# Attention, routed experts and a gated layer on one core: in the slots of the experts, only the splits of weights stand under conditions

## Chip, core and metric

One core of a Trainium2 chip runs the whole program in one launch. The metric is the device time of one execution in microseconds (us); lower is better.

## The reference

Three layers run one behind the other. The attention layer (batch 4, 8 heads, 576 positions, 64 per head) is causal softmax attention mixed with a memory term. Its output is taken as 2304 rows of 512 numbers and goes through a mixture of 8 experts, of which each row uses the one with the highest logit. The result goes through a gated layer with 1536 hidden columns. The part that the change touches is the second:

```python
for e in range(E):                       # E = 8
    mask = e_idx == e                    # e_idx = argmax(x @ w_gate)
    h = np.maximum(x[mask] @ w1[e], 0.0) # w1[e]: 512 x 1024
    ye = h @ w2[e]                       # w2[e]: 1024 x 512
    out[mask] = gate_w[mask, None] * eom[mask, e, None] * ye
```

## The kernel before

**Stages.** The program has a stage of attention and routing (to about 290 us in the profile), a stage of the experts (294 to 620 us) and a gated stage (to the end). The change is in the stage of the experts, in the method `experts`.

**Slots.** Rows are sorted by expert and cut into tiles of 128 rows, with padding where an expert's rows don't fill a tile. One tile is one slot; there are at least 18 (`FULL`) and at most 25 (`SLOTS`), and 23 run with these inputs. The program is written out for all slots; those from 18 on stand inside nested conditions (`more`). All slots use the same two weight tiles in on-chip memory, `W1` and `W2`. Which expert a slot belongs to is known only when the program runs: `another(s)` reads a bit that says whether slot s has another expert than slot s - 1. The condition is evaluated by every engine in its own queue. Here it holds for seven slots (1, 5, 6, 13, 14, 20 and 21, as the profile shows).

**Splits.** Products are made exact enough by splitting each operand into a high part (a copy in a shorter format, made by ACT) and a low part (the rest, made by DVE), and adding three products: high x high, high x low, low x high. An expert's weights are eight pieces of 128 x 1024: pieces 0 to 3 are `W1`, 4 to 7 are `W2`. `split_hi(n)` (line 1185, ACT) and `split_lo(n)` (line 1192, DVE) fill them from the tiles `raw0` to `raw7`; when both are done, the next expert's piece is loaded into the same `raw` tile from SP's queue (`load`, line 1162). So the weights of the next expert wait in `raw` while the present one is used.

**A slot.** `load_x` fetches the rows two slots ahead by an indirect transfer on POOL's queue (lines 1275, 1277). `layer1(n, ...)` is 12 products for half n of the hidden columns (line 1292); `relu(n)` writes `h` (DVE, line 1297); `h_turn(n)` transposes `h` on PE (line 1234) into `pT`; `h_keep(n, 0)` and `h_keep(n, 1)` make its high part (ACT, line 1306) and low part (DVE, line 1304). `layer2(s, n, ...)` is 12 products into `pY` (line 1313): m = 0 to 3 take the high parts of h and of the weights, 4 to 7 the low part of the weights, 8 to 11 the low part of h. `x_turn(s + 1)` and `x_keep(s + 1, ...)` (lines 1234, 1242, 1240) prepare the next slot's rows. `store_y` scales the result on ACT (line 1322) and stores it from SP's queue (line 1323). In slots 13 to 15 a finished tile of results in `yo` is also turned and kept for the gated stage.

**Conditions.** Each slot has two of them, each with an arm for a new expert and an arm for the same one (`either`). The arm `first_half_new` holds the splits of pieces 4 to 7, the keeping of the first half of h and the second ReLU, in one written order; `first_half` holds the same without splits. `second_half_new` and `second_half` do so for pieces 0 to 3 of the next slot's expert, the keeping of the second half of h and of the next x. An arm is one block: the engines run what stands in it in that order, and nothing from outside stands between.

**Gated conversions.** The weights of the gated layer come as 64-bit numbers. Six pieces (`SOON`) are converted during the slots, through the tile `early`, in three steps per piece: `small` (ACT, line 1204) and two conversions on DVE (1211, 1213); two more conversions (1215, 1217); a split (ACT 1229, DVE 1227) and the load of the next piece into `early`. Step k is in slot k, from slot 0 on.

**Order.** The stage is in an order written out by hand (`tc.manual_schedule`); each engine runs its own instructions in the order of the text, and waits where an operand or a buffer isn't ready.

Of the kernel before, what the change touches and what calls it, by code (L numbers as in the profile page):

```python
# [26 lines left out]
NE = 8  # L27
# [10 lines left out]
SOON = 6  # L38
SLOTS = 25
FULL = NT  # L40
# [1077 lines left out]
class Experts:  # L1118
# [126 lines left out]
    def experts(self, rt, gather):  # L1245
        tc, nc = self.tc, self.nc
        V, xn, ids = nc.vector, rt.xn, rt.ids
        with ExitStack() as ctx:
# [6 lines left out]
            xh, xl = (t[:, 0 : 4 * P].rearrange("p (c t) -> p c t", c=4) for t in self.yT)  # L1255
            hh, hl = ([t[:, (4 + 4 * n) * P : (8 + 4 * n) * P] for n in range(2)] for t in self.yT)
            pX, pH, pT, pY = self.ps
            marks = {}

            def value(t, lo, hi, **more):  # L1260
                return nc.values_load_multi_w_load_instructions(t, min_val=lo, max_val=hi, bass_reorder=False, **more)[1][0]
# [1 line left out]
            def only_sp(t, s, top):  # L1263
                return value(t[0:1, s : s + 1], 0, top, engines=[mybir.EngineType.SP])

            def another(s):

                k, b = divmod(s, BITS)
                if k not in marks:
                    marks[k] = value(rt.marks[0:1, k : k + 1], 0, 2**BITS - 1)  # L1270
                return ((marks[k] >> b) & 1) > 0
# [10 lines left out]
            def x_turn(s):  # L1282
                self.turn_rows(pX[s % 2], xn[s % 2])

            def x_keep(s, lo):
                self.keep_rows(pX[s % 2], (xh, xl), 0, lo)
# [9 lines left out]
            def relu(n):  # L1296
                nc.vector.tensor_scalar(h, pH[n], 0.0, None, ALU.max)  # L1297

            def h_turn(n):
                self.turn_rows(pT[n], h)  # L1300

            def h_keep(n, lo):
                if lo:
                    nc.vector.tensor_tensor(hl[n], pT[n], hh[n].bitcast(F32), ALU.subtract)  # L1304
                else:
                    nc.scalar.activation(hh[n], pT[n], AF.Copy)  # L1306
# [18 lines left out]
            def part(n):  # L1325
                self.split_hi(n)
                self.split_lo(n, V)

            def next_loads(s, ns):
                e = only_sp(rt.then, s, NE - 1)  # L1330
                for n in ns:
                    self.load(n, ds(e, 1))

            def first_half(s):

                h_keep(0, 0)
                h_keep(0, 1)
                relu(1)

            def first_half_new(s):  # L1340
                part(4)
                part(5)
                self.split_hi(6)
                h_keep(0, 0)
                h_keep(0, 1)
                relu(1)
                self.split_lo(6, V)
                part(7)
                next_loads(s, range(4, 8))

            def second_half(s):
                h_keep(1, 0)
                h_keep(1, 1)
                if s + 1 < SLOTS:
                    x_keep(s + 1, 0)
                    x_keep(s + 1, 1)

            def second_half_new(s):
                part(0)
                h_keep(1, 0)  # L1360
                h_keep(1, 1)
                part(1)
                x_keep(s + 1, 0)
                x_keep(s + 1, 1)
                part(2)
                part(3)
                next_loads(s + 1, range(4))

            def either(s, new, old, at):
                if not 0 < at < SLOTS:  # L1370
                    old(s)
                    return
                with tc.If(another(at)) as changed:
                    new(s)
                with changed.Else():
                    old(s)

            def slot(s):
                m, step = divmod(s, 3)
                turned = s - 13 if 13 <= s < 16 else None  # L1380
                load_x(s)
                layer1(0, range(12))
                relu(0)
                if m < SOON and step == 0:
                    self.small(m)
                layer1(1, range(6))
                h_turn(0)
                layer1(1, range(6, 12))
                either(s, first_half_new, first_half, s)
                if m < SOON:  # L1390
                    if step < 2:
                        self.convert(m, 2 * step)
                        self.convert(m, 2 * step + 1)
                    else:
                        self.split(m, 0)
                        self.split(m, 1, V)
                        if m + 1 < SOON:
                            self.load_mix(m + 1, self.early)
                layer2(s, 0, range(6))
                h_turn(1)  # L1400
                layer2(s, 0, range(6, 12))
                if s + 1 < SLOTS:
                    x_turn(s + 1)
                either(s, second_half_new, second_half, s + 1)
                if turned is not None:
                    self.turn_rows(pX[s % 2], self.yo[:, turned * DM : (turned + 1) * DM])
                    for i in range(2):
                        self.keep_rows(pX[s % 2], self.second, turned, i)
                layer2(s, 1, range(12))
                store_y(s)  # L1410
                if s in (11, 15):
                    self.load_rows(3 * (s == 15), 3)
# [309 lines left out]
```

## Time and profile before

| | |
|---|---|
| time, median of 3 runs | 1091.81 us (1091.31 to 1094.24) |
| the profiled execution's own time | 1091.38 us |
| its span in the profile | 1089.2 us |
| PE busy | 1009.7 us, 93% |
| DVE busy | 544.7 us, 50% |
| ACT busy | 456.8 us, 42% |
| POOL busy | 216.7 us, 20% |
| mean of the 16 DMA engines | 96 GB/s |

Times of single instructions and slots come from the one profiled execution; its span is the time from its first to its last instruction. PE is the engine of the products (PEld its loads of weights), DVE the vector engine, ACT the scalar engine, POOL the general one, SP the one that issues most transfers. An engine counts as busy while an instruction runs; conditions and register reads are not counted.

### The profile page before, as it was taken

Reading aid. Unit: us, or ns where it says so; the run is one execution under the profiler, and the core shown is the slowest. Engines: PE = TensorE matmul, PEld = TensorE weight load, DVE = VectorE, ACT = ScalarE, POOL = GpSimd, SP = SyncE. Lnnn points to the kernel's source line nnn. Section 1 sums busy time; section 2 is a strip of 40 time slices with the busy share of each in tenths; the row PEclk is TensorE's granted clock in tenths of the full one; section 3 lists DMA queues with packets and bytes.
Section 4 is the critical chain, followed back from the end, with each engine's and each line's share of the span. In section 5 each row is a group of like instructions: output and inputs, shape, how many; then the busy total and the mean of one; then the engine's idle time right before and its main releaser. Section 6 shows DMA issues by size and latency. Waiting matters only on the chain. (4 is left out here: it accounts for less than half of the span.)

```text
span 1089.2 us, 17370 instructions
## 1 busy us (share of the span) xinstructions
PE 1009.7 (93%) x5873; PEld 860.6 (79%) x5873; DVE 544.7 (50%) x1301; ACT 456.8 (42%) x1047; POOL 216.7 (20%) x353
## 2 busy tenths in 40 slices
PE   4889998999579889988998999999999999999997
PEld 3667776777457668867886799999999999999996
DVE  5887877774753653356437399952121121221112
ACT  4888777875342442245226265532211221221211
POOL 8786456530600100011000000000100100100101
PEclk9999999999689999999999999999999999999999
DMA  7667435230553471157218466500200100100000
GB/s 128 137 106 183 106 80 113 68 105 2 186 186 112 140 267 59 59 185 251 69 46 265 131 203 189 166 29 1 78 10 1 59 1 1 59 1 1 29 1 29
DMA packets 114840, 104.66 MB, mean 96 GB/s; under 512 B 71664, under 2 KB 89072, under 8 KB 114736
## 3 DMA queue, kind: packets, MB, share of 16 engines
q1 hardware_dynamic: 111264, 92.11, 30.2%
q0 software_dynamic: 3472, 11.30, 3.1%
q8 instruction: 48, 0.79, 0.3%
q14 instruction: 56, 0.46, 0.1%
HBM read 87.89 MB, written 15.50 MB: 95 GB/s over the span
## 5 line engine op out<-in xcount | busy, mean ns | idle before, releaser
L1529 DVE TENSOR_TENSOR G<-G,pT 128x384 f32<-128x384 f32 (+1 forms) x74 | 40.1, 542 | 247.7 <-PE pT L1515 241.2
L1313 PE MATMUL pY<-W,xh 128*128 128x512 f32 x368 | 103.2, 413 | 18.6 <-ACT W L1185 13.4
L1561 POOL DMA_INDIRECT out_dram<-yo,rows x18 | 17.5, 973 | 455.0 <-ACT yo L1557 364.0
L1536 ACT ACTIVATE Gh<-G 128x384 fp32r<-128x384 f32 (+1 forms) x74 | 38.2, 516 | 159.2 <-DVE G L1529 159.0
L1292 PE MATMUL pH<-W,xh 128*128 128x512 f32 x368 | 98.1, 399 | 2.8 <-ACT xh L1242 2.8
L1313 PEld LDWEIGHTS pY<-W,xh 128*128 128x128 f32 x368 | 66.2, 192 | 35.4 <-ACT W L1185 18.1
L1525 ACT ACTIVATE G<-pH 128x384 f32<-128x384 f32 x72 | 35.5, 492 | 124.5 <-PE pH L1515 124.4
L436 ACT ACTIVATE Sm<-Sm,mx 128x512 f32<-128x512 f32 (+3 forms) x144 | 83.7, 587 | 7.3 <-DVE mx L428 6.9
L1292 PEld LDWEIGHTS pH<-W,xh 128*128 128x128 f32 x368 | 70.0, 191 | 19.7 <-ACT xh L1242 3.2
L1306 ACT ACTIVATE xh<-pT 128x512 fp32r<-128x512 f32 x46 | 27.5, 598 | 122.5 <-PE pT L1234 106.4
L1297 DVE TENSOR_SCALAR h<-pH 128x512 f32<-128x512 f32 x46 | 31.5, 686 | 89.3 <-PE pH L1292 89.3
L1192 DVE TENSOR_TENSOR W<-raw,W 128x1024 fp32r<-128x1024 f32 x59 | 71.1, 1237 | 2.1 <-ACT W L1185 1.0
L428 DVE CUSTOM_DVE_ANT_0 Sm<-Sp,mask 128x512 f32<-128x512 f32 (+3 forms) x144 | 64.5, 482 | 14.3 <-PE T L480 6.9
L480 PE MATMUL T<-ident,Sm 128*128 128x128 f32 x400 | 61.9, 282 | 7.8 <-DVE xT L524 3.1
L318 ACT ACTIVATE pt<-T 128x512 f32<-128x512 f32 (+4 forms) x138 | 55.8, 447 | 30.1 <-PE T L480 28.8
L1185 ACT ACTIVATE W<-raw 128x1024 fp32r<-128x1024 f32 x60 | 60.6, 1050 | 0.3 <-ACT xh L1306 0.3
L480 PEld LDWEIGHTS T<-ident,Sm 128*128 128x128 f32 x400 | 43.9, 141 | 21.3 <-DVE xT L524 5.0
L1304 DVE TENSOR_TENSOR xl<-pT,xh 128x512 fp32r<-128x512 f32 x46 | 31.7, 690 | 57.1 <-ACT xh L1306 57.1
L1534 DVE TENSOR_TENSOR Gl<-G,Gh 128x384 fp32r<-128x384 f32 (+1 forms) x74 | 40.3, 545 | 32.7 <-ACT Gh L1536 32.7
L1292 PE MATMUL pH<-W,xl 128*128 128x512 f32 x184 | 56.7, 410 | 0.0
L1277 POOL DMA_INDIRECT xn<-x_dram,kept x23 | 24.1, 1047 | 155.3 <-PE pX L1234 154.8
L1313 PE MATMUL pY<-W,xl 128*128 128x512 f32 x184 | 50.4, 396 | 0.0
(355 smaller groups left out, 2254.2 us busy)
## 6 DMA issues: line engine op xcount, KB each, us to landing
raw<-in_moe_w_dram SPq DMA_DIRECT2D x68, 512.0 KB, 4.4
y_dram<-y SPq DMA_DIRECT2D x23, 256.5 KB, 5.3
vn<-in_v_dram SPq DMA_DIRECT2D x40, 128.0 KB, 2.6
raw<-in_moe_w_gate_dram SPq DMA_DIRECT2D x10, 512.0 KB, 3.8
raw<-in_moe_w_val_dram SPq DMA_DIRECT2D x10, 512.0 KB
raw<-in_moe_w_out_dram SPq DMA_DIRECT2D x10, 512.0 KB, 3.5
qn<-in_q_dram SPq DMA_DIRECT2D x32, 128.0 KB, 3.3
kn<-in_k_dram SPq DMA_DIRECT2D x32, 128.0 KB, 2.7
```

The source lines that it names most:

```text
L318: self.nc.scalar.activation(out, in_, AF.Copy)
L428: self.nc.vector.tensor_tensor_reduce(out=self.Sm[pi, n][:, k0:k1], in0=self.Sp[pi, c][:, j if n < 8 else si, 0 : k1 - k0], in1=mask, scal ...
L436: self.nc.scalar.activation(self.Sm[pi, n], self.Sm[pi, n], AF.Exp, scale=-1.0, bias=self.mx[pi, n][:, si : si + 1], accum_out=self.sums[p ...
L480: nc.tensor.transpose(T[:, o * 128 : (o + 1) * 128], self.Sm[pi, n][:, k0 : k0 + 128], self.ident)
L1185: self.nc.scalar.activation(self.hi_lo(n)[0], self.first[n] if n in self.first else self.raw[n], AF.Copy)
L1192: eng.tensor_tensor(lo[:, o : o + w], t[:, o : o + w], hi.bitcast(F32)[:, o : o + w], ALU.subtract)
L1292: nc.tensor.matmul(pH[n], lhsT=a[:, m % 4, :], rhs=self.W1[:, c : c + 512], start=(m == 0), stop=(m == 11))
L1313: nc.tensor.matmul(pY[s % 2], lhsT=a[n][:, k * P : (k + 1) * P], rhs=self.W2[:, c : c + 512], start=(n == 0 and m == 0), stop=(n == 1 and ...
L1525: nc.scalar.activation(G[g, f][0], pp[g, f, 0], AF.Sigmoid)
L1529: nc.vector.tensor_tensor(t, t, p, ALU.mult)
L1534: nc.vector.tensor_tensor(l, t, hi.bitcast(F32), ALU.subtract)
L1536: nc.scalar.activation(hi, t, AF.Copy)
```

## The change

- The splits alone stand under conditions, in five blocks per slot, without an else: piece 4 and the high parts of 5, 6, 7; the low parts of 5 and 6 and the loads of 4, 5, 6; the low part of 7 and its load; pieces 0 and 1 of the next expert with their loads; pieces 2 and 3 with theirs. Slot 0 has the last two of these alone.
- What belongs to h, x and the second ReLU stands outside the conditions.
- The next x is turned right behind the second turn of h, six products earlier.
- Step k of the gated conversions is in slot k + 1; slot 17 has the last two steps.
- The number of the expert to load is read by SP at the start of each slot, not inside the arms.

```diff
--- before.py
+++ after.py
@@ -1255,7 +1255,7 @@
             xh, xl = (t[:, 0 : 4 * P].rearrange("p (c t) -> p c t", c=4) for t in self.yT)
             hh, hl = ([t[:, (4 + 4 * n) * P : (8 + 4 * n) * P] for n in range(2)] for t in self.yT)
             pX, pH, pT, pY = self.ps
-            marks = {}
+            marks, following = {}, {}
 
             def value(t, lo, hi, **more):
                 return nc.values_load_multi_w_load_instructions(t, min_val=lo, max_val=hi, bass_reorder=False, **more)[1][0]
@@ -1326,82 +1326,81 @@
                 self.split_hi(n)
                 self.split_lo(n, V)
 
-            def next_loads(s, ns):
-                e = only_sp(rt.then, s, NE - 1)
+            def changed(s):
+
+                return tc.If(another(s)) if 0 < s < SLOTS else None
+
+            def loads(s, ns):
                 for n in ns:
-                    self.load(n, ds(e, 1))
-
-            def first_half(s):
-
+                    self.load(n, ds(following[s], 1))
+
+            def early(k):
+
+                m, step = divmod(k, 3)
+                if step == 0:
+                    self.small(m)
+                if step < 2:
+                    self.convert(m, 2 * step)
+                    self.convert(m, 2 * step + 1)
+                else:
+                    self.split(m, 0)
+                    self.split(m, 1, V)
+                    if m + 1 < SOON:
+                        self.load_mix(m + 1, self.early)
+
+            def slot(s):
+                ends, begins = 0 < s + 1 < SLOTS, 0 < s
+                turned = s - 13 if 13 <= s < 16 else None
+                if ends:
+                    following[s + 1] = only_sp(rt.then, s + 1, NE - 1)
+                load_x(s)
+                layer1(0, range(6))
+                if begins:
+                    with changed(s):
+                        part(4)
+                        for n in (5, 6, 7):
+                            self.split_hi(n)
+                layer1(0, range(6, 12))
+                relu(0)
+                layer1(1, range(3))
+                if begins:
+                    with changed(s):
+                        self.split_lo(5, V)
+                        self.split_lo(6, V)
+                        loads(s, (4, 5, 6))
+                layer1(1, range(3, 6))
+                h_turn(0)
                 h_keep(0, 0)
                 h_keep(0, 1)
+                layer1(1, range(6, 12))
                 relu(1)
-
-            def first_half_new(s):
-                part(4)
-                part(5)
-                self.split_hi(6)
-                h_keep(0, 0)
-                h_keep(0, 1)
-                relu(1)
-                self.split_lo(6, V)
-                part(7)
-                next_loads(s, range(4, 8))
-
-            def second_half(s):
+                layer2(s, 0, range(3))
+                if begins:
+                    with changed(s):
+                        self.split_lo(7, V)
+                        loads(s, (7,))
+                for k in ([] if not 0 < s < FULL else [s - 1] if s < FULL - 1 else range(s - 1, 3 * SOON)):
+                    early(k)
+                layer2(s, 0, range(3, 6))
+                if ends:
+                    with changed(s + 1):
+                        part(0)
+                        part(1)
+                        loads(s + 1, (0, 1))
+                h_turn(1)
+                if ends:
+                    x_turn(s + 1)
                 h_keep(1, 0)
                 h_keep(1, 1)
-                if s + 1 < SLOTS:
+                if ends:
                     x_keep(s + 1, 0)
                     x_keep(s + 1, 1)
-
-            def second_half_new(s):
-                part(0)
-                h_keep(1, 0)
-                h_keep(1, 1)
-                part(1)
-                x_keep(s + 1, 0)
-                x_keep(s + 1, 1)
-                part(2)
-                part(3)
-                next_loads(s + 1, range(4))
-
-            def either(s, new, old, at):
-                if not 0 < at < SLOTS:
-                    old(s)
-                    return
-                with tc.If(another(at)) as changed:
-                    new(s)
-                with changed.Else():
-                    old(s)
-
-            def slot(s):
-                m, step = divmod(s, 3)
-                turned = s - 13 if 13 <= s < 16 else None
-                load_x(s)
-                layer1(0, range(12))
-                relu(0)
-                if m < SOON and step == 0:
-                    self.small(m)
-                layer1(1, range(6))
-                h_turn(0)
-                layer1(1, range(6, 12))
-                either(s, first_half_new, first_half, s)
-                if m < SOON:
-                    if step < 2:
-                        self.convert(m, 2 * step)
-                        self.convert(m, 2 * step + 1)
-                    else:
-                        self.split(m, 0)
-                        self.split(m, 1, V)
-                        if m + 1 < SOON:
-                            self.load_mix(m + 1, self.early)
-                layer2(s, 0, range(6))
-                h_turn(1)
                 layer2(s, 0, range(6, 12))
-                if s + 1 < SLOTS:
-                    x_turn(s + 1)
-                either(s, second_half_new, second_half, s + 1)
+                if ends:
+                    with changed(s + 1):
+                        part(2)
+                        part(3)
+                        loads(s + 1, (2, 3))
                 if turned is not None:
                     self.turn_rows(pX[s % 2], self.yo[:, turned * DM : (turned + 1) * DM])
                     for i in range(2):
```

## Rows read from the trace of the kernel before

**Rows 1.** The page, part 1: busy time, share of the span, instructions.

```profile
PE 1009.7 (93%) x5873; PEld 860.6 (79%) x5873; DVE 544.7 (50%) x1301; ACT 456.8 (42%) x1047; POOL 216.7 (20%) x353
```

**Rows 2.** Waits of PE, 294 to 620 us: us in total, times, longest us.

```profile
PE pY L1313 <- ACT W L1185: 13.4, 14, 1.7
PE pT L1234 <- DVE W L1192: 9.3, 7, 1.4
PE pY L1313 <- ACT xh L1306: 5.2, 1, 5.2
```

**Rows 3.** Windows of slots 0, 1, 2, 4, 5, 6: length, engines busy, clock, DMA.

```profile
294.23:318.11 23.88, 17.00 (x61) 13.19 (x61) 10.93 (x22) 6.13 (x8) 2.25 (x4) 0.77 0.60 204
318.11:332.70 14.59, 12.95 (x62) 10.05 (x60) 9.10 (x11) 6.27 (x8) 1.52 (x3) 1.00 0.70 230
332.70:345.19 12.49, 12.49 (x61) 10.19 (x60) 3.96 (x6) 3.01 (x5) 1.26 (x3) 1.00 0.26 87
...
357.69:372.11 14.42, 12.74 (x62) 10.24 (x60) 9.01 (x11) 6.28 (x8) 1.66 (x3) 1.00 0.34 95
372.11:388.64 16.53, 13.23 (x61) 10.09 (x60) 12.95 (x14) 10.58 (x13) 1.44 (x3) 1.00 0.89 297
388.64:403.25 14.61, 12.99 (x62) 10.05 (x60) 8.57 (x11) 6.82 (x9) 1.26 (x3) 1.00 0.87 293
```

**Rows 4.** Timeline of PE in slot 3: start us, us, instruction.

```profile
349.40 0.60 PE L1234 MATMUL pT<-ident,h 128*128 128x128 f32 x4
...
352.63 0.60 PE L1234 MATMUL pT<-ident,h 128*128 128x128 f32 x4
...
354.81 2.10 PE L1313 MATMUL pY<-W,xh 128*128 128x512 f32 x8
356.75 1.10 PE L1313 MATMUL pY<-W,xl 128*128 128x512 f32 x4
```

**Rows 5.** Timeline of PE in slot 15: x, then `yo`, are turned.

```profile
520.89 0.60 PE L1234 MATMUL pX<-ident,xn 128*128 128x128 f32 x4
521.33 0.60 PE L1234 MATMUL pX<-ident,yo 128*128 128x128 f32 x4
521.69 2.10 PE L1313 MATMUL pY<-W,xh 128*128 128x512 f32 x8
```

**Rows 6.** Timeline of slot 5, in brackets what ended an idle time.

```profile
373.03 2.94 ACT L1185 ACTIVATE W<-raw 128x1024 fp32r<-128x1024 f32 x3
...
378.58 0.68 DVE L1297 TENSOR_SCALAR h<-pH 128x512 f32<-128x512 f32 x1
...
379.18 2.35 DVE L1192 TENSOR_TENSOR W<-raw,W 128x1024 fp32r<-128x1024 f32 x2
381.44 0.68 DVE L1227 TENSOR_TENSOR Wx<-cv_a,Wx 128x512 fp32r<-128x512 f32 x1
381.58 0.66 PE L1234 MATMUL pT<-ident,h 128*128 128x128 f32 x4 [1.33 <-DVE W L1192]
...
382.05 1.22 DVE L1192 TENSOR_TENSOR W<-raw,W 128x1024 fp32r<-128x1024 f32 x1
```

**Rows 7.** Timeline of ACT in slot 0, then windows of all engines there.

```profile
306.37 0.66 ACT L1204 ACTIVATE cv_a<-early 128x512 f32<-128x512 f32 x1 [12.20 <-DMA early<-in_moe_w_gate_dram]
...
306.00:310.00 4.00, 2.43 (x6) 1.94 (x7) 2.05 (x4) 2.09 (x3) 0.00 (x0) 0.50 0.00 0
310.00:312.00 2.00, 2.00 (x9) 1.62 (x8) 1.22 (x1) 0.61 (x2) 0.00 (x0) 0.51 0.00 0
```

**Rows 8.** Groups by line: busy us, mean ns of one, idle before.

```profile
L1217 DVE SCALAR_TENSOR_TENSOR cv_a<-early,cv_a 128x512 int32<-128x512 int32 x6 | 4.2, 692 | 0.2
...
L1211 DVE TENSOR_SCALAR cv_a<-cv_a 128x512 f32<-128x512 f32 x26 | 10.5, 418 | 0.0
```

**Rows 9.** The page, part 6: transfers, KB each, median us to landing.

```profile
raw<-in_moe_w_dram SPq DMA_DIRECT2D x68, 512.0 KB, 4.4
```

**Rows 10.** Waits, 619 to 624 us: PE's queue at a condition not taken.

```profile
PE pH L1515 <- PEq L1416: 0.5, 1, 0.5
```

## The prediction

> **What bounds the kernel now.** I read the page first, then PE's waits in the stage of the experts, then that stage cut into slots, then slots 3, 5 and 0 instruction by instruction. The page shows PE busy 93% of the span [rows 1], so a gain can only come from time in which PE stands still. The profiled execution took 1091.38 us, 2.2 us more than its span of 1089.2; the median of the runs shown is 1091.81, 0.4 above. My sum is made against 1091.4.
>
> The stage runs from 294.2 to 620.1 us: 23 slots. A slot in which nothing changes takes 12.49 us, and PE is busy in all of it [rows 3]: it cannot become shorter unless work is removed, and none is. The slots that are longer are slot 0 and those around the seven changes of expert (the changes are at slots 1, 5, 6, 13, 14, 20 and 21).
>
> PE's waits in the stage [rows 2] have three causes that this change can touch:
> - 14 waits, 13.4 us, of the second-layer products for an ACT instruction of line 1185, and 7 waits, 9.3 us, of the transposes of h for a DVE instruction of line 1192. That is two of the first and one of the second for each change.
> - one wait of 5.2 us for line 1306, in slot 0.
>
> Slot 5 shows what the first kind is. The ReLU writes h at 378.58, two splits of weights follow, and the transpose that reads h, and no weight, starts at 381.58, right behind the end of the splits [rows 6]. So PE does not wait for its operand; it waits for the end of the conditional arm that the operand was made in. That is the mark of it: the releaser is a line whose result is not read.
>
> What it costs is better read from lengths of slots than from idle time, since PE also drains and refills: slots 4, 5 and 6 are 1.93, 4.04 and 2.12 us over 12.49 [rows 3], 8.1 for two changes, 4.04 for one. Slots 12 to 14 and 19 to 21 repeat this, and slots 0 and 1 hold one more change: 7 x 4.04 = 28.3 us. In slot 13 a turn of `yo` fills 0.44 us of it [rows 5], which leaves 27.9.
>
> Slot 0 is 23.88 us long [rows 3]. ACT stands at line 1204 until 306.37, 12.2 us, for the transfer into `early` [rows 7]; behind it in ACT's queue is the copy of h that PE waits 5.2 us for. [...] So the gated conversion costs 7.4 us.
>
> **The change, part by part.**
>
> *h and x kept outside the conditions.* The copies and subtractions of h and x and the second ReLU now stand outside every arm, so their readers need not wait for splits that stand in the same arm. Gain: at most the 27.9 us. A split itself still has to be done before its first reader, so I lay the new order of slot 5, the fullest (it ends one change and begins another), against the places where a slot without waits wants things: the transposes of h at 4.2 and 7.4 us, the last twelve products at 9.6, and the four of them that read the low half of h at 11.6 [rows 4], counted from 345.19.
> ACT: a split costs 0.98 [rows 6]. The first starts 0.9 into the slot, as now [rows 6]; it does 4, 5, 6, 7 to 4.8, then the copy of h to 5.4; wanted at 6.0 (the turn at 4.2, then six products of 0.24). Then splits 0 and 1 to 7.9, h to 8.5, x to 9.1, splits 2 and 3 to 11. Nothing is late.
> DVE: a split costs 1.17, a small step (ReLU, subtraction) 0.6 [rows 6]. Splits 2 and 3 of the slot before reach to about 1.4 by the same steps, and ACT's part of split 4 to 1.9; split 4 to 3.1; ReLU to 3.7, in time for 4.2; splits 5 and 6 to 6.1; subtraction of h and ReLU to 7.3, wanted 7.4 less about 0.1 for the handover: 0.15 late; split 7 to 8.5; two conversions at 0.69 [rows 8] to 9.9; splits 0 and 1 to 12.2; the subtraction of h to 12.9. That is wanted at 11.6, and PE has by then lost nothing else: about 1.5 us late with the handover. DVE's busy time agrees: 12.95 us in slot 5 [rows 3], less one conversion step and plus two, 13.6, against 12.49 of PE.
> Slot 13 has the two shorter conversions, 0.42 each [rows 8], and the turn of `yo`: 1.5 - 0.54 - 0.44, some 0.6 late there, and, since DVE also subtracts the kept rows, 0.6 in slot 14. Slot 20 has no conversion: 0.2. The 0.15 at the second ReLU comes seven times: 1.0. Left over: 1.5 + 0.6 + 0.6 + 0.2 + 1.0 = 3.9.
>
> *Five conditions instead of two, without an else.* 45 conditions become 112 (now two in a slot and one in slot 0, then five and two), and every engine passes each. In the trace DVE leaves an arm and starts the conversion behind it at 381.44 without a gap, and enters the next arm 0.61 later, the spacing of one step [rows 6]; and PE shows no idle time in slot 2, though it passes two conditions there [rows 3]. So I take nothing. Cover: on DVE and ACT the instruction still running, and in unchanged slots the room that the six products behind each turn leave (1.4 us, of which the copy of h takes 0.6); on PE the products queued. The other bound is the one row in which PE's queue itself is the releaser, a condition not taken with nothing behind it: 0.5 us [rows 10]. Without cover the 67 added ones would cost 67 x 0.5, some 34 us.
> [...]
>
> *Conversions from slot 1.* The same instructions, one slot later; the load into `early` keeps its place, so the wait of 12.2 us falls away with the 7.4 us. Later loads of `early` are still issued a slot ahead of their reader. What is late next is slot 17, which now holds two steps: ACT must wait for DVE's two conversions (about 8.6), split, and copy h behind that, about 0.9 us after PE wants it. In slot 0 the first read of the marks by PE and ACT moves to the middle of the slot, where less lies ahead of it: 0.4 taken, between nothing and twice the 0.5 of [rows 10], since no row shows it by itself.
>
> *The turn of x behind the second turn of h.* The same four transposes, six products earlier, so POOL may fetch the next x that much earlier; nothing waits for it. Two turns in a row cost 0.44 + 0.36 where `yo` follows x [rows 5]: up to 0.08 us more than one by itself, against one change-over less; 0.02 taken, 0.4 over 22 slots.
>
> *Loads and SP.* The same eight loads for each change, each behind its own split, as before; SP reads the next expert in every slot, but its address is wanted only when split 4 is done, 3 us into the slot. A load lands 4.4 us after issue [rows 9], and has 8 us or more until its split, even between slots 5 and 6. Nothing.
>
> **The sum.** 27.9 + 7.4 = 35.3 to be had; less 3.9 (DVE), 0.9 (slot 17), 0.4 (marks), 0.4 (turns) = 29.7. 1091.4 - 29.7 = 1061.7 us. The products of the gated stage keep their order and are only shifted.
>
> **The rivals.**
> - *DVE carries the arms.* In changed slots DVE has no slack any more, so an uncovered arm costs there what it costs. Seven changes, five arms each, up to 0.5 us: up to 17.5 us, 1062 to 1079. For it: DVE's 13.6 against 12.49. Against it: the gapless 381.44. Chance 0.17.
> - *The waits stay.* If the condition itself, and not the place of the copy within it, holds the reader back, only slot 0 gains: 1084. For it: every wait of this kind in the trace stands behind an arm. Against it: the delay ends exactly with a split. Chance 0.07.
> - *The branches bind PE (the other side).* If PE's queue has no lead at the added conditions, each costs 0.5 us: 1061.7 + 34 = 1096. It decides from 29.7 / 67 = 0.44 us per condition. For it: the added ones stand three products behind a wait, where the lead is shortest. Against it: the 45 of now cost nothing that shows. Chance 0.07. [...]
>
> **How the numbers follow.** The forecast holds 1056 to 1067 (from all 35.3 recovered to 5 us of small waits): chance 0.66. The rivals take 0.17, 0.07 and 0.07; 0.03 is left for no change. The range 1056 to 1076 takes in the forecast and most of the first rival. A measurement tells about 0.3% (3 us) from no change: faster 0.90, same 0.03, slower 0.07.
>
> **What the profile after would show.** Right: waits of PE for lines 1185 and 1192 nearly gone, slots 4 and 6 at about 12.6, slot 5 at about 14.1 with PE waiting for DVE's subtraction, slot 0 at about 15 (23.88 - 7.4 - 1.93 + 0.4) with no wait at 1204 and no fall of the granted clock inside it, and 12.5 in the rest. Wrong, if unchanged slots are longer than 12.6 (branches), if slots 5, 13 and 20 reach 15 or more (DVE's arms), or if transposes of h still end their wait with a split.

## The result, and the profile after

The changed kernel takes 1060.53 us (median of 4 runs, 1058.03 to 1061.86), the kernel before, run beside it, 1092.28 (4 runs, 1091.31 to 1094.24). The ratio is 0.9703, its 95% interval 0.9684 to 0.9723. The profiled execution of the changed kernel took 1060.34 us, 1058.6 of them span. First its page, part 1, which answers to [rows 1]; PE's instructions are as many as before:

```profile
PE 1005.1 (95%) x5873; PEld 861.6 (81%) x5873; DVE 544.7 (51%) x1301; ACT 455.0 (43%) x1047; POOL 221.2 (21%) x353
```

The waits of PE over the whole stage, which answer to [rows 2]:

```profile
PE pH L1292 <- ACT xh L1242: 3.0, 1, 3.0
PE pY L1313 <- DVE xl L1304: 1.2, 2, 0.9
```

The 14 waits for line 1185, the 7 for line 1192 and the one for line 1306 are gone. The first of the two rows stands at the very start of the stage, for the first turned x; the kernel before has it too, with 2.8 us. The other is new: PE waits in slots 5 and 13 for DVE's subtraction of h.

Windows of slots 0, 1, 2, 4, 5 and 6 of the changed kernel, as in [rows 3]:

```profile
296.53:311.20 14.67, 14.67 (x61) 11.98 (x61) 9.34 (x20) 5.58 (x7) 2.47 (x4) 0.84 0.84 294
311.20:323.68 12.48, 12.48 (x62) 10.26 (x60) 9.04 (x12) 6.73 (x9) 1.26 (x3) 1.00 0.95 320
323.68:336.17 12.49, 12.49 (x61) 10.23 (x60) 4.75 (x7) 2.37 (x4) 1.26 (x3) 1.00 0.15 51
...
348.67:361.17 12.50, 12.50 (x61) 10.23 (x60) 7.36 (x10) 6.83 (x9) 1.26 (x3) 1.00 0.22 81
361.17:374.89 13.72, 12.78 (x61) 10.12 (x60) 13.13 (x16) 10.07 (x12) 2.77 (x3) 1.00 0.96 328
374.89:387.38 12.49, 12.49 (x61) 10.20 (x60) 10.09 (x12) 6.68 (x9) 2.12 (x3) 1.00 0.91 319
```

All 23 slots (us; slots that are not listed lie between 12.46 and 12.50 in both kernels):

| slot | 0 | 1 | 4 | 5 | 6 | 12 | 13 | 14 | 15 | 17 | 19 | 20 | 21 | 22 |
|---|---|---|---|---|---|---|---|---|---|---|---|---|---|---|
| before | 23.88 | 14.59 | 14.42 | 16.53 | 14.61 | 14.43 | 16.53 | 15.03 | 12.94 | 12.50 | 14.42 | 16.55 | 14.61 | 12.69 |
| after | 14.67 | 12.48 | 12.50 | 13.72 | 12.49 | 12.46 | 13.40 | 13.19 | 12.93 | 12.89 | 12.47 | 12.48 | 12.49 | 12.67 |

The stage went from 326.1 to 293.1 us: 9.2 less in slot 0 and 23.8 less in the other slots. The span shrank by 30.6 only, since the stage began at 296.5 instead of 294.2; of that more below. The gated stage has its old length.

Slot 5 after, which answers to [rows 6] (timeline of DVE and PE, in brackets what ended an idle time):

```profile
367.78 0.68 DVE L1297 TENSOR_SCALAR h<-pH 128x512 f32<-128x512 f32 x1
368.38 1.22 DVE L1192 TENSOR_TENSOR W<-raw,W 128x1024 fp32r<-128x1024 f32 x1
...
368.62 0.60 PE L1234 MATMUL pT<-ident,h 128*128 128x128 f32 x4
...
370.84 2.36 DVE L1192 TENSOR_TENSOR W<-raw,W 128x1024 fp32r<-128x1024 f32 x2
...
373.12 0.68 DVE L1304 TENSOR_TENSOR xl<-pT,xh 128x512 fp32r<-128x512 f32 x1
...
373.86 1.20 PE L1313 MATMUL pY<-W,xl 128*128 128x512 f32 x4 [0.94 <-DVE xl L1304]
```

The same pair as before, the ReLU and then a split of weights: but the transposes of h now start 0.24 us into the split, and not behind its end. Lower down is the new limit: the splits of pieces 0 and 1 fill DVE until 373.1, the subtraction of h comes behind them, and the last four products wait 0.94 us for it.

In slot 0 no instruction waits for the transfer into `early` any more. From 306 to 312 us the granted clock was 0.50 before, where PE stood still for 5.2 us until 307.57 [rows 2, 7]; in the changed kernel PE is busy without a gap, and the same windows show 1.00:

```profile
306.00:308.00 2.00, 2.00 (x15) 1.74 (x14) 2.00 (x2) 1.54 (x4) 0.06 (x1) 1.00 0.12 35
308.00:310.00 2.00, 2.00 (x10) 1.64 (x9) 2.00 (x4) 1.76 (x2) 1.12 (x1) 1.00 0.90 240
310.00:312.00 2.00, 2.00 (x10) 1.61 (x9) 1.76 (x2) 0.54 (x1) 0.00 (x0) 1.00 0.97 375
```

The first six products of the second layer in slot 0 took 2.93 us at 0.50 before and 1.56 at 1.00 after (timelines of PE, before, then after):

```profile
307.57 2.93 PE L1313 MATMUL pY<-W,xh 128*128 128x512 f32 x6 [5.20 <-ACT xh L1306]
```

```profile
304.75 1.56 PE L1313 MATMUL pY<-W,xh 128*128 128x512 f32 x6
```

What slot 0 still takes over the 12.48 us of an unchanged slot is the clock too. PE stood still for 3.0 us before the stage, and the clock is at 0.50 when it begins at 296.53 and rises at about 301.2; half of these 4.6 us is 2.3, and slot 0 is 2.2 longer:

```profile
294.00:296.00 2.00, 0.00 (x0) 0.00 (x0) 1.89 (x1) 0.12 (x1) 1.93 (x2) 0.50 0.64 170
...
298.00:300.00 2.00, 2.00 (x6) 1.63 (x5) 0.53 (x6) 0.00 (x0) 0.06 (x1) 0.50 0.86 300
300.00:302.00 2.00, 2.00 (x8) 1.55 (x8) 0.29 (x1) 0.00 (x0) 0.25 (x2) 0.71 0.97 339
```

### The profile page after: what moved, and what is told of

The parts are those of the page before. It is cut to its first block, busy times and chain, and to the rows that moved or that the text cites. A ratio compares the mean times of both kernels' runs of the same rounds, so it can differ in the third digit from the quotient of the medians.

```text
span 1058.6 us, 18515 instructions
## 1 busy us (share of the span) xinstructions
PE 1005.1 (95%) x5873; PEld 861.6 (81%) x5873; DVE 544.7 (51%) x1301; ACT 455.0 (43%) x1047; POOL 221.2 (21%) x353
## 5 line engine op out<-in xcount | busy, mean ns | idle before, releaser
L1313 PE MATMUL pY<-W,xh 128*128 128x512 f32 x368 | 99.0, 401 | 0.1
L318 ACT ACTIVATE pt<-T 128x512 f32<-128x512 f32 (+4 forms) x138 | 55.9, 448 | 30.9 <-PE T L480 29.7
L399 PE MATMUL Sp<-kz,qT 64*128 64x512 f32 (+3 forms) x384 | 46.7, 357 | 1.6 <-DVE mx L428 1.5
```

Of the source, the lines that this page charges most:

```text
L318: self.nc.scalar.activation(out, in_, AF.Copy)
L399: nc.tensor.matmul(Sp[:, j, 0:n], lhsT=q[r, a, c * 128 : (c + 1) * 128], rhs=kz[r, k, 0:n], start=(p_ == 0), stop=(p_ == 2), skip_group_ch ...
L1313: nc.tensor.matmul(pY[s % 2], lhsT=a[n][:, k * P : (k + 1) * P], rhs=self.W2[:, c : c + 512], start=(n == 0 and m == 0), stop=(n == 1 and ...
```

## The experiments

E1, E3 and E4 put one part of the change into the kernel before, the others change one thing in the changed kernel or run a kernel again. "Stage" is the length of the stage of the experts in the profile, from its first product to half a microsecond before the first product of the gated stage. Ratios are to the kernel before, run on the same chip; the interval is 95%. E1 to E4 ran on one chip, E5 to E8 on another and E9 to E11 on a third; the kernel before took 1091.79, 1091.06 and 1091.16 us there.

| kernel | median us (lowest to highest, runs) | ratio, interval | stage us |
|---|---|---|---|
| before, first profile | 1092.28 (1091.31 to 1094.24, 4) | | 326.1 |
| after, first profile | 1060.53 (1058.03 to 1061.86, 4) | 0.9703, 0.9684 to 0.9723 | 293.1 |
| E1 conversions a slot later | 1085.03 (1083.58 to 1086.19, 5) | 0.9938, 0.9917 to 0.9959 | 318.8 |
| E3 first half alone | 1078.45 (1077.43 to 1080.94, 4) | 0.9889, 0.9861 to 0.9917 | 310.5 |
| E4 second half alone | 1079.03 (1078.62 to 1079.81, 4) | 0.9889, 0.9865 to 0.9914 | 312.3 |
| E2 after, conversions from slot 0 | 1061.82 (1058.65 to 1065.92, 4) | 0.9729, 0.9691 to 0.9768 | 295.9 |
| E8 after, a ReLU back in an arm | 1063.89 (1063.53 to 1065.24, 4) | 0.9755, 0.9738 to 0.9771 | 298.8 |
| E5 after, ten conditions per slot | 1062.56 (1062.25 to 1063.41, 4) | 0.9739, 0.9723 to 0.9756 | 296.3 |
| E6 after, x turned later | 1059.99 (1058.90 to 1060.48, 4) | 0.9712, 0.9696 to 0.9728 | 292.9 |
| E7 after, conversion steps moved | 1057.21 (1055.67 to 1059.09, 4) | 0.9695, 0.9679 to 0.9711 | 290.5 |
| E9 after again, beside E10 | 1059.88 (1058.52 to 1060.86, 5) | 0.9708, 0.9688 to 0.9728 | 293.5 |
| E10 E7 again, beside E9 | 1056.99 (1056.34 to 1058.36, 5) | 0.9684, 0.9664 to 0.9703 | 291.1 |
| E11 before again | 1092.72 (1 run) | | 324.0 |

**E1: the conversions alone.** The kernel before, with step k of the gated conversions in slot k + 1.

```diff
-                m, step = divmod(s, 3)
+                ks = [] if not 0 < s < FULL else [s - 1] if s < FULL - 1 else range(s - 1, 3 * SOON)
...
-                if m < SOON and step == 0:
-                    self.small(m)
+                for k in ks:
+                    if k % 3 == 0:
+                        self.small(k // 3)
...
-                if m < SOON:
+                for k in ks:
+                    m, step = divmod(k, 3)
```

> The kernel before with one part of the change: the gated conversions begin in slot 1 (slot 17 has two steps). Theory: ACT's wait at the first conversion goes, and with it PE's 5.2 us and the 2.2 us lost at the lower clock: 7.4 less up to 0.9 for slot 17, so about 1085 us, slot 0 at about 16.5 us, the slots around changes as before (14.4, 16.5, 14.6). Rival one: the transfer is waited for by something else in slot 0, and the time stays at 1092. Rival two: the clock was not part of the price, and only 5.2 us go: 1087.

Slot 0 of E1 as a window, and two rows of its waits of PE in the stage:

```profile
296.16:312.32 16.16, 14.48 (x61) 11.61 (x61) 10.16 (x20) 5.70 (x7) 2.36 (x4) 0.89 0.85 293
```

```profile
PE pY L1313 <- ACT W L1185: 13.4, 14, 1.7
PE pT L1234 <- DVE W L1192: 9.8, 7, 1.7
```

Slot 0 lost 7.7 us (23.88 to 16.16); the time fell by 6.8. The waits at the changes of expert stayed, all 21 of them: the two parts of the gain are apart.

**E3 and E4: one half of the slot each.** The kernel before with only the first, or only the second, of its two conditions broken up. The turn of x and the conversions keep their places.

```diff
E3
-                layer1(0, range(12))
+                layer1(0, range(6))
+                if s:
+                    with tc.If(another(s)):
+                        part(4)
+                        for n in (5, 6, 7):
+                            self.split_hi(n)
+                layer1(0, range(6, 12))
...
-                either(s, first_half_new, first_half, s)
+                relu(1)
+                if s:
+                    with tc.If(another(s)):
+                        self.split_lo(7, V)
+                        next_loads(s, (7,))
E4
+                if s + 1 < SLOTS:
+                    with tc.If(another(s + 1)):
+                        part(0)
+                        part(1)
+                        next_loads(s + 1, (0, 1))
                 h_turn(1)
...
-                either(s, second_half_new, second_half, s + 1)
+                second_half(s)
+                if s + 1 < SLOTS:
+                    with tc.If(another(s + 1)):
+                        part(2)
+                        part(3)
+                        next_loads(s + 1, (2, 3))
```

> The kernel before with the new form of the first condition alone: splits 4 to 7 in three conditions without an else, the keeping of the first half of h and the second ReLU outside. Theory: the 2.1 us of the first half go at each of seven changes, 14.8 in all less small waits: 1077 to 1079; slots 1 and 6 at 12.5 to 12.7, slot 4 stays at 14.4, and no transpose of h waits for line 1192. Rival: the condition itself holds the readers back, and the time stays at 1092 or, with one more condition after a wait, rises.

> The kernel before with the new form of the second condition alone: splits 0 to 3 of the next expert in two conditions without an else, the keeping of the second half of h and of x outside. Theory: the 1.93 us go at each of seven changes, 13.1 in all (0.44 was filled by a turn of yo), less up to 1.5 where DVE is full in slots 5, 13 and 20: 1079 to 1081; slots 4 and 12 at 12.5 to 12.7, slots 1 and 6 stay at 14.6. Rival: as for the first half, 1092.

The waits of PE that are left, of E3, then of E4:

```profile
PE pY L1313 <- ACT W L1185: 11.3, 7, 1.7
```

```profile
PE pT L1234 <- DVE W L1192: 8.0, 6, 1.3
...
PE pT L1234 <- DVEq L1401: 1.4, 1, 1.4
PE pY L1313 <- ACT W L1185: 1.2, 4, 0.3
PE pY L1313 <- ACTq L1401: 0.9, 3, 0.3
```

Each half took away the waits behind its own arm and left those of the other: in E3 the seven long ones behind the second arm, in E4 seven behind each engine's part of the first (1.3 us each for DVE, 0.3 for ACT; a row with DVEq or ACTq is a wait of the same kind, put down to the engine's queue). Both also keep the wait for line 1306 in slot 0 (2.6 and 4.5 us), and E3 shows one new wait of 0.7 us for line 1192, in slot 13. In E3 slots 1, 6 and 21 fell to about 12.5 and slots 4, 12 and 19 stayed at 14.4; in E4 it is the other way round (12.5 in 4, 12 and 19, and 14.6 in 1, 6 and 21). Each is worth 1.1% of the time by its ratio, 12 us; the medians are 13.3 and 12.8 us apart. E1, E3 and E4 together are 0.62 + 1.11 + 1.11 = 2.84% (31.0 us) by the ratios and 32.9 us by the medians; the whole change took 2.97% and 31.75 us. Within the intervals the parts add up. E3's stage is also 2.3 us shorter in slot 0, which its edit doesn't touch (21.57; E11 has 21.68).

**E8: is it the place within the arm?** The changed kernel with one instruction, the second ReLU, put back into an arm, ahead of the split of piece 7 that already stood behind it; where the condition doesn't hold, it stands alone in the other arm. DVE's order is the same.

```diff
-                relu(1)
                 layer2(s, 0, range(3))
                 if begins:
-                    with changed(s):
+                    with changed(s) as arm:
+                        relu(1)
                         self.split_lo(7, V)
                         loads(s, (7,))
+                    with arm.Else():
+                        relu(1)
+                else:
+                    relu(1)
```

> The changed kernel with the second ReLU alone put back into a condition, ahead of the low split 7 and its load, and by itself into the else. Theory: the transpose of h then waits for the end of the arm, the split, which it does not read: 0.7 to 1 us in each of the seven changed slots, 4 to 6 us in all, 1065, with line 1192 named as the releaser. Rival: only data hold a reader back; the ReLU stands ahead of the split, and nothing changes: 1060.5.

Slot 1 of E8 (timeline of DVE and PE), then its waits of PE for `pT` in the stage:

```profile
314.99 0.68 DVE L1297 TENSOR_SCALAR h<-pH 128x512 f32<-128x512 f32 x1
315.59 1.22 DVE L1192 TENSOR_TENSOR W<-raw,W 128x1024 fp32r<-128x1024 f32 x1
...
316.86 0.66 PE L1234 MATMUL pT<-ident,h 128*128 128x128 f32 x4 [0.83 <-DVE W L1192]
```

```profile
PE pT L1234 <- DVE W L1192: 5.3, 6, 0.9
...
PE pT L1234 <- DVEq L1390: 0.9, 1, 0.9
```

The wait is back, with the same releaser as in [rows 2]: the turn of h begins when the split is done, 1.9 us after the ReLU began, where the changed kernel needed 0.84 (367.78 to 368.62). The stage grew by 5.7 us. The time, 1063.89 us, is 3.9 over that of E6, which ran on the same chip and has the slots of the changed kernel; the ranges of the two don't overlap. It grew by less than the stage, since the stage began at 293.9 in E8 and at 296.7 in E6. Slots 1, 6, 20 and 21 grew by 1.1 each, 14 by 0.9, 13 by 0.6; slot 5 kept its 13.72: its last four products, which read DVE's later subtraction, start 12.69 us into it in E8 as in the changed kernel. Slots whose condition is not taken did not grow (those of 12.46 to 12.50 now take 12.45 to 12.54). So in these runs a reader of something made in an arm is held to the end of that arm, and only where the arm with the split is taken.

The trace also holds the counters (semaphores) by which engines wait for each other, and they show how this comes about. Each of DVE's instructions in the slots shown raises one and the same counter at its end, and the transposes wait for a value of it. In slot 1 of E8 the ReLU raised it at 315.68, and PE stayed still; the split raised it at 316.81, and PE started at 316.86. So the awaited value is the one at the end of the arm. In the 15 slots of E8 in which the arm isn't taken, the ReLU that stands alone in the other arm raises the counter by a step of its own; where a condition has no other arm and isn't taken, DVE's queue raises it by itself, in the changed kernel in all 77 such places that skip work of DVE. The sizes of these steps are not in the trace; they fit a program that brings the counter to the same value at the end of a condition whichever way it went, so that one value serves the reader. Then the delay comes from how the program counts, and not from DVE: the ReLU was done.

**E5: what a condition costs.** The changed kernel with each of its five conditions cut in two: 112 more, with the same work in them.

```diff
                     with changed(s):
                         part(4)
+                    with changed(s):
                         for n in (5, 6, 7):
                             self.split_hi(n)
...
                     with changed(s):
                         self.split_lo(5, V)
+                    with changed(s):
                         self.split_lo(6, V)
                         loads(s, (4, 5, 6))
```

The other three are cut alike.

> The changed kernel with each of its five conditions cut in two: the same splits and loads, ten conditions in a slot, 112 more that every engine passes. Theory: they are covered, so no more than 1 us: 1060 to 1062, slots without a change at 12.47 to 12.5. Rival: a condition costs an engine 0.5 us each, 56 us: up to 1116, and the slots without a change grow to 15. In between would show as some tenths in each of the unchanged slots. [...]

The stage grew by 3.2 us, more than the 1 us that was allowed for: 0.03 us for each added condition. More than half of the slots show nothing. Slot 17, with two conversion steps and no change of expert, grew most, from 12.89 to 13.60, then slots 12 and 13 by 0.4 and slot 5 by 0.3. Slot 17 shows the price of a condition that is not taken, on DVE and ACT. First the changed kernel, one condition ahead of each of these instructions, then E5, two in a row (timelines of slot 17):

```profile
520.40 0.69 DVE L1297 TENSOR_SCALAR h<-pH 128x512 f32<-128x512 f32 x1
521.24 0.69 DVE L1215 SCALAR_TENSOR_TENSOR cv_a<-early,cv_a 128x512 int32<-128x512 int32 x1 [0.15 <-DVEq L1379]
...
523.50 0.60 ACT L1306 ACTIVATE xh<-pT 128x512 fp32r<-128x512 f32 x1 [0.17 <-ACTq L1386]
```

```profile
522.18 0.69 DVE L1297 TENSOR_SCALAR h<-pH 128x512 f32<-128x512 f32 x1
...
523.37 0.69 DVE L1215 SCALAR_TENSOR_TENSOR cv_a<-early,cv_a 128x512 int32<-128x512 int32 x1 [0.50 <-DVEq L1381]
...
526.00 0.60 ACT L1306 ACTIVATE xh<-pT 128x512 fp32r<-128x512 f32 x1 [0.55 <-ACTq L1392]
...
526.65 2.13 PE L1313 MATMUL pY<-W,xh 128*128 128x512 f32 x8 [0.82 <-ACT xh L1306]
```

DVE's queue is the releaser, 0.15 us with one condition and 0.50 with two; on ACT 0.17 and 0.55. In E5 PE waits 0.82 us behind that; the two increases, 0.35 and 0.38, are about the 0.71 by which the slot grew.

The records of the queues, which the timeline leaves out, show why the second in a row costs more. A condition is two register operations and a branch (45, 45 and 56 ns on DVE), and, where it skips work of DVE, the raising of its counter (21 ns). In the changed kernel the first three ran from 520.41 to 520.63, under the ReLU, which ended at 521.09; only the raising of the counter, which stands at 521.13, waited for it. In E5 the second condition's register operations began at 523.01, behind the first one's raising of the counter at 522.91, and its branch ended at 523.22: nothing covered them.

In the other slots that grew, PE's own queue is late; in slot 13 PE also waits 0.25 us longer for DVE. In slots 1, 4, 5, 6, 8, 12, 13 and 16 the second transposes of h start 0.06 us after the second of two conditions in that queue, and 0.28 to 0.61 us after the product ahead of them, against 0.24 in the changed kernel. In slots 2, 3 and 10 the branch is done a few hundredths of a us earlier, and they start on time. Why the queue has less lead in the eight stays open.

**E2: the conversions back in slot 0.** The changed kernel with step k in slot k.

```diff
-                for k in ([] if not 0 < s < FULL else [s - 1] if s < FULL - 1 else range(s - 1, 3 * SOON)):
+                for k in [s] if s < 3 * SOON else []:
                     early(k)
```

> The changed kernel with this part undone: step k of the conversions in slot k again. Theory: ACT stands at the first conversion until the transfer lands, some 12 us into slot 0; behind it are two splits and the second copy of h, which PE then gets about 3 us late, and the clock may fall once more: 3 to 5 us over the changed kernel, 1064 to 1066. Rival one: it costs the full 7.4 us as before, 1068. Rival two: the new order hides it, 1060.5.

ACT in slot 0 of E2, and the row of PE's waits for it:

```profile
302.61 0.60 ACT L1306 ACTIVATE xh<-pT 128x512 fp32r<-128x512 f32 x1 [6.45 <-PE pT L1234]
306.85 0.66 ACT L1204 ACTIVATE cv_a<-early 128x512 f32<-128x512 f32 x1 [3.64 <-DMA early<-in_moe_w_gate_dram]
```

```profile
PE pY L1313 <- ACT xh L1306: 2.5, 1, 2.5
```

Slot 0 became 3.5 us longer (18.18), not 7.7 as in the old order. The transfer lands as late as before, but the first copy of h now stands ahead of the waiting conversion in ACT's queue, not behind it, so PE has work for longer. Behind the 2.5 us in which PE stood still the granted clock was 0.50 once more, from 309.7 to 313.1. Slots 5 and 17 gave back 0.7 and 0.4, as other steps fall on them, slot 13 took 0.3 more, and the stage was 2.8 longer. The time, 1.3 us over the changed kernel's, is less than was expected, and its runs lie 7 us apart: it can't be told from the changed kernel by the time. By these two profiles the later start of the conversions is worth 2.8 us of the stage in the new order.

**E6: the turn of x.** The changed kernel with x turned at its old place, six products later.

```diff
                 h_turn(1)
-                if ends:
-                    x_turn(s + 1)
                 h_keep(1, 0)
                 h_keep(1, 1)
+                layer2(s, 0, range(6, 12))
                 if ends:
+                    x_turn(s + 1)
                     x_keep(s + 1, 0)
                     x_keep(s + 1, 1)
-                layer2(s, 0, range(6, 12))
```

> The changed kernel with the next x turned at its old place, behind all twelve products. Theory: the move is worth nothing, slots without a change stay within 0.05 us of 12.47 and the time at 1060.5, plus or minus 1. Rival: the earlier turn lets ACT and DVE keep x sooner, which the full slots 5, 13 and 20 need: 1 to 3 us more without it, seen as longer slots there.

1059.99 us, every slot within 0.04 us of the changed kernel's but slot 0 (14.30; the clock was low for its first 3.8 us, not 4.6). The move is worth nothing either way.

**E7, E9, E10, E11: less work for DVE where an expert ends and another begins.** The changed kernel with no conversion step in slots 5 and 13 and one instead of two in slot 17; slots 8, 10 and 16 take two.

```diff
+STEPS = {1: (0,), 2: (1,), 3: (2,), 4: (3,), 6: (4,), 7: (5,), 8: (6, 7), 9: (8,), 10: (9, 10), 11: (11,), 12: (12,), 14: (13,), 15: (14,), 16: (15, 16), 17: (17,)}
...
-                for k in ([] if not 0 < s < FULL else [s - 1] if s < FULL - 1 else range(s - 1, 3 * SOON)):
+                for k in STEPS.get(s, ()):
                     early(k)
```

> The changed kernel with no step of the conversions in slots 5 and 13 and one in slot 17 (two steps each in slots 8, 10 and 16 in their place; the slots are those that change with these inputs). Theory: what is left over PE's own time in the stage is DVE's load, so slot 5 falls from 13.72 to 12.5 us, slot 13 from 13.40 to 12.9 to 13.0 and slot 17 from 12.89 to 12.5: 2 to 2.4 us less, 1058. Rival: these slots wait for something else, and keep their lengths.

Slot 5 of E7 as a window:

```profile
357.20:369.69 12.49, 12.49 (x62) 10.21 (x61) 11.95 (x14) 10.28 (x13) 3.36 (x3) 1.00 0.93 325
```

DVE is busy for 11.95 us of that slot instead of 13.13, PE waits nowhere in it, and slot 17 is 12.50; slots 13 and 14 keep 12.92 and 13.06, almost all of which is the turn of `yo`. E7 was the fastest, so it was run again beside the changed kernel, with the kernel before for a second profile of the start of the stage.

> The changed kernel once more, beside the next one on the same chip. Theory: 1060.5, plus or minus 1.5; the stage of the experts 293.1 us long within 0.5, while the place where it starts, which lay between 293.9 and 296.7 us in the profiles so far with the same instructions ahead of it, may move by 2 us. Rival: the start is later in this kernel than in the one before for a reason in the change, and lies at 296.5 again.

> The kernel with the steps of the conversions moved out of slots 5 and 13 and one step in slot 17, once more. Theory: 2.6 us less than the changed kernel beside it, as the lengths of the slots say: 1057.9. Rival: the difference of the medians so far came from other places, and the two agree within 1 us.

> The kernel before once more, for its profile: the stage of the experts 326.1 us long, its start anywhere from 293.9 to 296.7 us if the start is not a matter of the change; at 294.2 again if it is.

E10 is 2.9 us faster than E9 beside it (1056.99 against 1059.88, and the ranges don't overlap); the stage is 2.4 shorter. E9 and E11 were also to tell whether the changed stage begins later. It does not: with the same instructions ahead of it, the stage began between 293.9 and 297.6 us in all the profiles, at 294.2 and 297.6 in the two of the kernel before, at 296.5 and 296.7 in those of the changed one. In E11 slot 0 took 21.68 us, not 23.88, and ACT's wait for `early` ended at 307.99 instead of 306.37: the stage began 3.4 later and the transfer came only 1.6 later.

## Why the prediction was right, step by step

**The waits behind arms (27.9 us).** Right, in size and in cause. The mark that the prediction went by, a releaser whose result is not read, was enough: E3 and E4 each removed what stood behind their own arms, and E8 made the wait again by moving one instruction across the edge of an arm. Lengths of slots were the better measure: of the 8.1 us by which slots 4 to 6 were longer before, 6.6 are time in which PE was idle, and 1.5 stand in its busy time, which is 12.74, 13.23 and 12.99 us there against 12.49 in slot 2 [rows 3]. In slots 1 to 22 the stage lost 23.8 us; slot 0, which holds the second-half arm of the first change of expert, lost 1.5 from E1 to the changed kernel (16.16 to 14.67, with the clock low for its first 3.6 and 4.6 us); and 2.4 us are left over (below). That makes 27.7.

**Slot 0 (7.4 us).** Right as a step: E1 measured 7.7 in the slot and 6.8 in the time. Of the 7.4, 5.2 are PE's wait [rows 2]; the other 2.2 were the author's estimate, half of the 4.4 us that PE was busy at a clock of 0.50 [rows 7]. No run shows the 2.2 by themselves; an estimate from the six products above, 2.93 us instead of 1.56, is 2.1. But the size hangs on when the stage begins, which the prediction took from one profile: between the two profiles of the kernel before slot 0 differs by 2.2 us, so that this term fits as well as it does is in part luck. And E2 shows that the same wait, put into the new order, costs the stage only 2.8: part of the 7.4 would have come from the order alone.

**DVE's left-overs (3.9) and slot 17 (0.9): over-sized.** Measured over the unchanged length of each slot: 1.23 in slot 5, 0.47 and 0.26 in slots 13 and 14 beyond the turn of `yo`, 0.40 in slot 17, nothing in slot 20 and nothing for the seven second ReLUs: 2.4 against 4.8. The order that the prediction laid out for DVE was good to about 0.3 us: counted from 361.17, the splits of pieces 0 and 1 end at 12.0 where 12.2 was worked out, the subtraction at 12.6 instead of 12.9. The second turn of h starts 7.45 us into slot 5 (368.62), as it does in a slot without a change (7.44, [rows 4]), so the handover that was to make it 0.15 late, seven times, is not seen. E7 shows that the conversion steps were what did not fit: with none in slots 5 and 13 and one in 17, what was left in slots 5 and 17 went away.

**Conditions (taken as nothing).** Right for this change: its unchanged slots take 12.46 to 12.50 us with five conditions, as with two. It is not quite nothing: the uncovered ones in slot 17 cost 0.15 on DVE and 0.17 on ACT, and part of that slot's 0.40 is theirs; twice as many cost 3.2 us (E5), because other work covers nearly all of them.

**The marks (0.4) and the turns of x (0.4).** The first can't be told: slot 0 took 14.67 and 15.09 us in the two profiles, 14.95 were forecast, and its length goes with the clock. In the seven profiles in which nothing waits for `early` there (the changed kernel's two, E5 to E8 and E10) the clock is low for the first 3.5 to 5.6 us of slot 0, and its 14.20 to 15.09 us are 12.48 plus half of that, within 0.2. The prediction had no term for this and took it over with the 23.88 of its one profile. The second is nothing, by E6.

**The sum.** 29.7 us were forecast. The medians differ by 31.75, the stages of the first two profiles by 33.0, those of E9 and E11 by 30.5. The 2 us that the medians give beyond the sum have the size of the left-overs that did not come (4.8 less 2.4), but that they are these is not shown: 0.9 of them come from the kernel before, 1092.28 in the runs beside the changed kernel where the sum was made against 1091.4, and the start of the stage alone moves by more than 2 us between profiles.

**The rivals.** "The branches bind PE" needed 0.44 us for a condition; E5 shows 0.03, though with ten in a slot PE's queue does lose its lead in eight slots. "The waits stay" is ruled out by the waits of the changed kernel, and E8 shows the edge of the arm to be what matters. "DVE carries the arms" has its place right, slots 5 and 13, but not its price: a split in a taken arm follows the step ahead of it without a gap (367.78, then 368.38 in slot 5), and in E7 slot 5 holds the same five arms in 12.49 us.

What stays open is why the stage begins up to 3.7 us later in some profiles than in others, and why PE's queue has less lead in some slots than in others.

## What to carry to other kernels

Look in the list of waits for releasers whose result the waiting instruction does not read; where such an instruction ends a conditional arm, take everything that others read out of that arm and leave under the condition only what depends on it. Then lay the engine that the arm loads against the times at which its other results are wanted, and move work that has no hurry out of the slots in which two such loads meet (here the conversion steps of slots 5 and 13 and one of slot 17's two: 2.9 us in E10). The table of steps in E7 fits these inputs only: it is written for slots 5 and 13, in which an expert ends and another begins here. A conversion that waits for a transfer cost less here behind a copy that the bound engine needs than ahead of it (2.8 us of the stage in E2, against the 7.3 that E1 took out of it).

## What the runs showed beyond that

One condition not taken cost DVE 0.15 and ACT 0.17 us in slot 17, two in a row 0.50 and 0.55: the queue runs the first one's branch while the engine still works, and the second one's when it is done. In this program a condition that skips work of DVE also makes up DVE's counter (in all 77 such places of the changed kernel), and in E8 the reader behind a condition waits for the counter at its end (316.81 us in slot 1, where PE starts at 316.86). And the start of the stage moves by 3.7 us (293.9 to 297.6) between profiles with the same instructions ahead of it, so a wait for a transfer at its beginning changes its length with it.
